# Spectral filter plus expert lookup on one core: the last tile in one piece, and a new list of ranks

## The chip, the cores and the metric

The kernel runs on one core of a Trainium2 chip. The metric is the device time of one execution in microseconds (us); the program must give the reference's output. Times of several runs are given as a median with the lowest and the highest. The profile is of one execution.

## The reference

The input `x` has 2048 rows of 576 columns. The output is `x` plus two branches.

- Branch A is a global spectral filter: a layer norm over the columns, a real two-dimensional Fourier transform over rows and columns, a product with complex weights `w_r + i w_i`, and the inverse transform.
- Branch B is an expert lookup with product keys. Each row is multiplied with query weights for 32 heads; each head's query has two halves of 128, and each half is compared with 8 keys; the best key of each half gives one of 64 experts. With one candidate per head the softmax is 1. The head adds `gelu(x . u[e]) * v[e]`.

```
xn = layernorm(x)
y  = irfft2(rfft2(xn) * (w_r + 1j * w_i))
q  = x @ w_q                      # 32 heads, 2 x 128 each
e  = argmax(q1 @ k1.T) * 8 + argmax(q2 @ k2.T)
out = x + y + sum over heads of gelu(x . u[e]) * v[e]
```

## The kernel before

All transforms are matrix products on TensorE. The rows are split as 64 x 32, and `x` lies in SBUF as 16 tiles of 128 partitions and 576 columns (`XN`, and as `XD` with the columns as two halves). The stages are these.

- Forward: `ln` and `folds` make the normed and folded tiles, `dft128` the first part of the row transform into `AB` and `ABL`.
- Query weights: 32 pieces of `w_q` are loaded and contracted with the keys (`fold_part`), so that the scores come straight from `x`.
- For each of 16 groups: `d_fwd`, `s_fwd`, `s_mul`, `s_inv` (column transform, rest of the row transform, product with the weights `Wt`, inverse row transform). Between them, for each of 8 pairs of tiles, the lookup: `x_t`, `scores`, `route`, `combine`. `combine` writes the expert weights of two tiles into `CAT` (the profile calls it by its storage, `MT`).
- Last stage: for each of 16 tiles `d_inv` gives the inverse column transform (11 + 3 matrix products, folds on ACT, VectorE and GpSimd), and `fin` does the rest: 16 products into one PSUM tile of 128 x 576 (the inverse row transform of 64 with weights `RT` in f32, and `CAT` times `vS` in f16), one VectorE sum with `x` that writes back to `XD`, and two output transfers of 64 partitions, each 144 KB. One f32 product shows as two records in the profile, so a tile has 8 f32 and 12 f16 records.

The output transfers of `fin` go to SyncE's queue; for tiles 13 to 15 the second one goes to ACT's queue. The last tile is different: it is worked in two column halves of 144 of each 288, each with its own PSUM tile, 16 products, one sum and two transfers of 72 KB.

The order of the work is not the order of the program text. Every operation is first recorded in a planner (`_Plan`). `prepare` finds the dependencies, and `forward` then runs a list schedule: at each step the engine that can start earliest takes, of its ready operations, the one with the lowest number in `RANK`, which has one number for each recorded operation (consecutive TensorE calls of one stage may be one operation). Costs of operations come from `cost`: a transfer from SyncE costs

```
            return max(450.0, out.shape[0] * n * size_of(out.dtype) / 400.0), self.land
```

in nanoseconds of its queue, and one from ACT 450. The planner also places the PSUM tiles. Then `issue` emits all operations in that order, from one line (L546), so that almost every instruction of the profile bears this line. `RANK` begins at line 138.

Of the kernel before, what the change touches and what calls it, by code (L numbers as in the profile page):

```python
# [32 lines left out]
def _consts():  # L33
# [168 lines left out]
)  # L202
# [362 lines left out]
def _body(ctx, tc, nc, plan, a, out):  # L565
# [590 lines left out]
    @staged  # L1156
    def fin(t, y):
        x = XD[:, t]
        if t == 15:
            for n, z in enumerate((slice(0, 144), slice(144, 288))):  # L1160
                p = PS("bc"[n])
                for k in range(4):
# [145 lines left out]
```

## Time and profile before

| | |
|---|---|
| median of 3 runs | 213.25 us (212.79 to 215.01) |
| the profiled execution | 213.16 us |
| its span, first to last instruction | 211.4 us |
| TensorE matmul busy | 189.9 us, 90% |
| VectorE busy | 183.6 us, 87% |
| ScalarE (ACT) busy | 129.9 us, 61% |
| GpSimd (POOL) busy | 110.4 us, 52% |
| mean granted TensorE clock | 0.996 |
| output transfers | 28 of 144 KB from SyncE, 2 from ACT; 2 of 72 KB from each |

In the profile's rows PE is the matrix product on TensorE, PEld its weight load, DVE is VectorE, SPq and ACTq are the queues of SyncE and ACT that issue transfers. A row of the timeline has the start, the time to the end of the merged group, the engine, the operation, the tiles (out<-in) and the count. A row of a DMA view has the queue or the engine, the count, the size and the time from issue to landing. The output is called `out_dram`; the last stage's input tiles are `A` and `MT`, its sums write `XN`.

### The profile page before, as it was taken

How to read it: one execution, taken by the hardware profiler on the slowest of the kernel's cores; microseconds unless marked ns; L12 is line 12 of the kernel's file. 1: busy time of each engine (PE TensorE's matmuls, PEld its weight loads, DVE VectorE, ACT ScalarE, POOL GpSimd, SP SyncE). 2: the span in 40 equal slices, each digit the busy share in tenths (PEclk: the TensorE clock that was granted, in tenths of full speed). 3: DMA queues.
4: the chain of work that ended last, by engine and by line, in shares of the span. 5: the costliest groups of instructions: out<-in, count | busy, mean ns of one | idle time of the engine just before them, and what ended most of it. 6: DMA issues, size and time to landing. Idle time of an engine off the chain costs nothing.

```text
span 211.4 us, 6192 instructions
## 1 busy us (share of the span) xinstructions
PE 189.9 (90%) x2408; PEld 130.6 (62%) x2408; DVE 183.6 (87%) x430; ACT 129.9 (61%) x305; POOL 110.4 (52%) x153
## 2 busy tenths in 40 slices
PE   0187799999999999999999999999989999999980
PEld 0175467778767566746666645465644787878850
DVE  2999899955986977988899999999999999999880
ACT  2378998899956884954948974693826622422310
POOL 5526363523088431592518535874836338768750
PEclk9999999999999999999999999999999999999998
DMA  6999999999999999997355062010100001484755
GB/s 197 367 419 410 421 414 416 375 374 399 414 424 407 414 392 401 446 400 302 87 175 158 35 198 67 0 40 0 40 0 2 3 3 28 116 198 113 171 132 150
DMA packets 17453, 48.13 MB, mean 228 GB/s; under 512 B 2192, under 2 KB 8848, under 8 KB 16656
## 3 DMA queue, kind: packets, MB, share of 16 engines
q1 hardware_dynamic: 16848, 47.30, 61.3%
q10 hardware_dynamic: 576, 0.44, 0.7%
q8 instruction: 19, 0.31, 0.6%
q14 instruction: 10, 0.08, 0.1%
HBM read 43.01 MB, written 4.72 MB: 226 GB/s over the span
## 4 chain that ended last, share of the span: by engine, by line
PE 61%; DVE 28%; issue 3%; ACT 2%; DMA 2%; POOL 1%; DVEq 0%; POOLq 0%
PE banks L546 61%; DVE t L546 6%; DVE MT L546 4%; DVE st L546 4%; DVE A L546 3%; DVE w L546 2%; DVE AB L546 2%; DMA XN<-in_x_dram 2%; DVE ABL L546 1%; DVE rr L546 1%; DVE mx L546 1%; DVE mm__96 L546 1%; DVE mv L546 1%; DVE mxr L546 1%; DVE al L546 1%
## 5 line engine op out<-in xcount | busy, mean ns | idle before, releaser
L546 PE MATMUL banks<-MU,xT 128*128 128x512 f16 x192 | 45.6, 379 | 0.6 <-DVE w L546 0.6
L546 PE MATMUL banks<-c,AB 128*128 128x145 f16 (+2 forms) x320 | 37.6, 251 | 0.0
L546 PEld LDWEIGHTS <-xT 128*128 128x128 f16 x224 | 21.1, 98 | 24.5 <-issue 1.5
L546 POOL TENSOR_TENSOR y<-t,t 128x289 f32<-128x289 f32 x32 | 23.8, 766 | 18.4 <-DVE t L546 12.8
L546 POOL TENSOR_TENSOR A<-t 128x287 f32<-128x287 f32 (+2 forms) x42 | 26.2, 641 | 8.8 <-DVE t L546 4.7
L546 POOL TENSOR_TENSOR yh<-y,yh 128x578 f16<-128x578 f32 x16 | 21.2, 1328 | 9.5 <-DVE mxr L546 3.0
L546 POOL TENSOR_TENSOR xT<-xf,xT 128x640 f16<-128x640 f32 x10 | 14.3, 1428 | 22.3 <-DVE A L546 8.2
L546 DVE SCALAR_TENSOR_TENSOR t<-banks,wx,Wt 128x578 f32<-128x578 f32 x32 | 24.6, 811 | 1.4 <-PE banks L546 1.4
L546 PE MATMUL banks<-Rs,yl 128*99 128x128 f32 x64 | 11.0, 305 | 13.0 <-ACT Rs L546 11.2
L546 PE MATMUL banks<-w,KP 128*32 128x288 f32 x256 | 20.5, 415 | 0.3 <-DMA w<-in_wq_dram 0.3
L546 ACT ACTIVATE AB<-banks 128x512 f32<-128x512 f32 (+1 forms) x32 | 18.8, 591 | 0.7 <-PE banks L546 0.7
L546 PE MATMUL banks<-c,ABL 99*128 99x289 f16 (+1 forms) x64 | 18.9, 296 | 0.0
L546 PE MATMUL banks<-Rs,A 128*128 128x128 f32 x128 | 18.7, 297 | 0.0
L546 PEld LDWEIGHTS banks<-c,AB 128*128 128x128 f32 x128 | 18.1, 190 | 0.7
L546 PEld LDWEIGHTS banks<-Rs,yl 128*99 128x99 f32 x64 | 8.3, 180 | 16.5 <-ACT Rs L546 11.9
L546 ACT ACTIVATE yh<-banks 128x290 f32<-128x290 f32 (+1 forms) x16 | 7.2, 457 | 18.2 <-PE banks L546 18.2
L546 PEld LDWEIGHTS banks<-Rs,A 128*128 128x128 f32 x128 | 17.1, 209 | 1.9 <-issue 1.4
L546 DVE TENSOR_REDUCE MT<-w 128x128 bf16<-128x896 bf16 (+1 forms) x16 | 18.1, 1142 | 0.1
L546 POOL TENSOR_TENSOR t<-XN 128x289 f32<-128x289 f32 x14 | 11.5, 824 | 11.4 <-DVE rr L546 3.2
L546 PEld LDWEIGHTS <-AB 128*128 128x128 f16 x192 | 17.0, 146 | 0.1
L546 ACT ACTIVATE A<-banks 128x578 f16<-128x578 f32 (+1 forms) x16 | 10.4, 650 | 8.8 <-PE banks L546 8.8
L546 PE MATMUL banks<-A,s 64*64 64x289 f16 (+1 forms) x320 | 15.6, 336 | 0.0
(131 smaller groups left out, 413.1 us busy)
## 6 DMA issues: line engine op xcount, KB each, us to landing
w<-in_wq_dram SPq DMA_DIRECT2D x32, 576.0 KB, 6.4
xf<-in_xT_dram SPq DMA_DIRECT2D x16, 320.0 KB, 5.2
Wt<-in_W_dram SPq DMA_DIRECT2D x8, 578.0 KB, 6.5
out_dram<-XN SPq DMA_DIRECT2D x28, 144.0 KB, 2.5
XN<-in_x_dram SPq DMA_DIRECT2D x3, 1154.0 KB, 10.3
s<-in_s_dram SPq DMA_DIRECT2D x16, 192.0 KB, 3.5
XN<-in_xd_dram SPq DMA_DIRECT2D x2, 1152.0 KB, 8.3
XN<-in_xd_dram SPq DMA_DIRECT2D x1, 2304.0 KB, 14.0
```

The source lines that it names most:

```text
L546: ins = fn(*[x.place() if isinstance(x, _Ps) else x for x in args], **{k: x.place() if isinstance(x, _Ps) else x for k, x in kw.items()}).ins
```

## The change

`fin` loses its branch for the last tile, so that tile 15 is worked like tile 14: one PSUM tile, 16 products, one sum, and two transfers of 144 KB, the first from SyncE and the second from ACT. This removes four recorded operations of the planner (1273 become 1269), and `RANK` is replaced by a list of 1269 other numbers. The words of the change say that output transfers are counted at their traced issue times in the order; `cost` itself is the same before and after, so of this only the new list is in the code.

```diff
 RANK = (
-    1031, 1229, 1032, 1219, 1241, 1243, 1242, 1033, 1245, 730, 572, 810, 562, 803, 319, 320, 329, 377, 707,
...
+    755, 784, 785, 862, 1225, 1234, 1233, 1238, 1224, 570, 578, 569, 568, 1127, 515, 767, 462, 769, 1084,
...
 )
...
     def fin(t, y):
         x = XD[:, t]
-        if t == 15:
-            for n, z in enumerate((slice(0, 144), slice(144, 288))):
-                p = PS("bc"[n])
-                for k in range(4):
-                    for h in range(2):
-                        hs = slice(64 * h, 64 * h + 64)
-                        for c in range(2):
-                            cs, ds = slice(64 * c, 64 * c + 64), slice(288 * c + z.start, 288 * c + z.stop)
-                            w, m = ((RT[hs], y[hs, ds]) if k == 0 else
-                                    (CAT[hs, t, 64 * (k // 3):64 * (k // 3) + 64], vS[hs, k % 2 ^ 1, ds]))
-                            P.matmul(p[cs, h, z], w, m, start=(k == 0), stop=(k == 3), tile_position=(64 * h, 64 * c))
-                V.scalar_tensor_tensor(x[:, :, z], p[:, :, z], sc[:, 11:12], x[:, :, z], op0=OP.mult, op1=OP.add)
-                for c in range(2):
-                    (A if c else Q).dma_start(os[t, c, :, :, z], x[64 * c:64 * c + 64, :, z])
-            return
         p = PS("bc"[t % 2])
         for k in range(4):
             for h in range(2):
...
```

124 rows, old and new, of the table RANK are left out of this document.

## The prediction

> **What bounds the kernel now.** I read the page first, then the busy time by stage, then the end of the chain of waits, and last the instructions and transfers of the final 8 us one by one.
>
> ```profile
> span 211.4 us, 6192 instructions
> PE 189.9 (90%) x2408; PEld 130.6 (62%) x2408; DVE 183.6 (87%) x430; ACT 129.9 (61%) x305; POOL 110.4 (52%) x153
> ...
> q8 instruction: 19, 0.31, 0.6%
> ```
>
> The stage table gives, after the stretch, its length, each engine's busy time (with its instructions), the granted clock, the DMA share and GB/s.
>
> ```profile
> 0.00:31.25 31.25, 17.94 (x138) 13.71 (x138) 26.04 (x103) 21.66 (x60) 15.71 (x36) 1.00 0.95 371
> 31.25:118.05 86.80, 86.06 (x1087) 59.16 (x1088) 71.96 (x161) 66.50 (x143) 40.66 (x44) 1.00 0.89 344
> 118.05:175.30 57.25, 56.17 (x653) 33.84 (x651) 56.87 (x110) 33.66 (x82) 31.56 (x39) 1.00 0.11 33
> 175.30:205.10 29.80, 29.71 (x532) 23.85 (x532) 27.94 (x58) 8.07 (x23) 22.45 (x35) 1.00 0.53 126
> 205.10:211.40 6.30, 0.00 (x0) 0.00 (x0) 0.78 (x2) 0.00 (x0) 0.00 (x0) 0.86 0.60 164
> ```
>
> Until 31.25 us the loads and VectorE set the pace. From there to 205.10 TensorE is idle for only 0.74 + 1.08 + 0.09 = 1.91 us by the second to fourth rows, and from 118.05 VectorE is idle for only 0.38 + 1.86 = 2.24 us. After 205.10 come 6.30 us in which TensorE does nothing and the DMA engines are 60% busy. So there are two places where an edit can act: a body in which two engines are nearly full, and a tail of transfers.
>
> ```profile
> 175.32 28.86 PE banks L546 x492
> ...
> 204.21 0.46 DVE XN L546
> ...
> 204.95 0.51 DVE XN L546
> 205.46 0.42 DVEq L1304
> ```
>
> The chain runs through the last stage on TensorE and then over the last sums (L546 is the planner's emitting line, so every instruction bears it; the tile names tell them apart). It stops at 205.88, 5.5 us before the span's end, because the view follows no transfer to its landing. Therefore the transfers have to be read one by one.
>
> **The change part by part.** *Product.* These are the last whole tile (t = 14, the first two rows) and the two halves of t = 15:
>
> ```profile
> 203.14 0.66 PE L546 MATMUL banks<-A,c 64*64 64x288 f32 x8
> 203.62 0.55 PE L546 MATMUL banks<-vS,MT 64*64 64x288 f16 x12
> 203.99 0.43 PE L546 MATMUL banks<-A,c 64*64 64x144 f32 x8
> 204.23 0.37 PE L546 MATMUL banks<-vS,MT 64*64 64x144 f16 x12
> 204.42 0.42 PE L546 MATMUL banks<-A,c 64*64 64x144 f32 x8
> 204.67 0.37 PE L546 MATMUL banks<-vS,MT 64*64 64x144 f16 x12
> ```
>
> The whole tile lasts from 203.14 to 204.17, 1.03 us; the halves last from 203.99 to 205.04, 1.05 us. Put in place of the halves, a whole tile ends at 203.99 + 1.03 = 205.02. Twenty matmul records and twenty weight loads go, worth 0.02 us here. ACT and SyncE issue nothing but these transfers at the end (no engine but VectorE is busy after 205.10), so no compute waits behind an issue.
>
> *Sum.* VectorE's rows are the sum of t = 14 and the two half sums:
>
> ```profile
> 204.21 0.82 DVE L546 SCALAR_TENSOR_TENSOR XN<-banks,sc,XN 128x576 f32<-128x576 f32 x1
> ...
> 204.95 0.93 DVE L546 SCALAR_TENSOR_TENSOR XN<-banks,sc,XN 128x288 f32<-128x288 f32 x2
> ```
>
> The halves end at 204.95 + 0.93 = 205.88. The sum of t = 14 starts 0.04 after its product's end at 204.17, so a whole sum would start at 205.06 (VectorE is free at 205.03) and end at 205.06 + 0.82 = 205.88. The difference is nothing. What is lost is the head start of the first half: the chain has it end at 204.95 + 0.51 = 205.46, 0.42 before the second.
>
> *Transfers.* The issues of the tail, with the two queues' times:
>
> ```profile
> 203.71 0.61 SPq L546 DMA_DIRECT2D out_dram<-XN  x1
> 204.21 0.67 ACTq L546 DMA_DIRECT2D out_dram<-XN  x1
> ...
> 205.07 1.90 SPq L546 DMA_DIRECT2D out_dram<-XN  x1
> 205.74 1.24 ACTq L546 DMA_DIRECT2D out_dram<-XN  x1
> 207.06 0.56 SPq L546 DMA_DIRECT2D out_dram<-XN  x1
> 207.08 0.83 ACTq L546 DMA_DIRECT2D out_dram<-XN  x1
> 207.92 0.53 SPq L546 DMA_DIRECT2D out_dram<-XN  x1
> ```
>
> The last four of these are the quarters of t = 15. Two issues, the 1.90 and the 1.24, run long and both end near 206.97. The times from issue to landing, of narrow windows around the issues at 203.14, 203.71, 205.06 with 205.07, and 207.92, are:
>
> ```profile
> out_dram<-XN SPq DMA_DIRECT2D x1, 144.0 KB, 2.3
> ...
> out_dram<-XN SPq DMA_DIRECT2D x1, 144.0 KB, 4.1
> ...
> out_dram<-XN ACTq DMA_DIRECT2D x1, 144.0 KB, 4.0
> out_dram<-XN SPq DMA_DIRECT2D x1, 144.0 KB, 4.4
> ...
> out_dram<-XN SPq DMA_DIRECT2D x1, 72.0 KB, 2.5
> ```
>
> A transfer that meets nothing takes 2.3; the next one lands only at 203.71 + 4.1 = 207.8. Then the landings come at a fixed pitch: four more whole transfers by 205.07 + 4.4 = 209.5 (0.42 each), and four quarters by 207.92 + 2.5 = 210.4 (0.23 each). After that the program needs 211.4 - 210.4 = 1.0 to end. The tail is thus a backlog and not a last transfer. What starts it shows in the DMA queues of the window 204.9 to 205.6:
>
> ```profile
> q1 hardware_dynamic: 141, 0.14, 87.3%
> q8 instruction: 1, 0.02, 12.3%
> ```
>
> One instruction packet takes 0.123 x 16 x 0.7 = 1.38 us on one of the 16 engines, in the middle of the transfers, and every transfer needs its share of that engine. By the page there are 19 such packets of 0.31 MB; over 2408 + 2408 TensorE instructions that is 64 bytes each, so I read them as TensorE's instruction stream, one packet per 253 instructions.
>
> Now the price. Two whole transfers in place of four quarters, behind the same backlog: 2 x 0.42 against 4 x 0.23, that is 0.84 against 0.92, a gain of 0.1. That is the small end. If the lost head start of 0.42 counts in full, the tail loses 0.42 - 0.08 = 0.3. The large end has no packet in the way: the transfers land from 203.71 + 2.3 = 206.0 on at a pitch of 0.42, seven of them, so the last by 206.0 + 6 x 0.42 = 208.5; but the two of t = 15, issued at 205.95, can't land before 205.95 + 2.3 = 208.25 and, one pitch later, 208.7. That is 1.7 earlier than 210.4. Between these I take a gain of 0.9: the packet still comes (40 instructions fewer are a sixth of its pitch), but two of the five whole transfers in the backlog, those of t = 12 or 13, are placed ahead of it (2 x 0.42), and the quarters' 0.1 goes.
>
> The Trainium skill, "DMA: Bandwidth & Descriptors", section "Anatomy of one DMA — SWDGE (gpsimd) path", fits a transfer's time on the GpSimd path by about 2.0 us plus its bytes over 436 GB/s. For 144 KB this gives an estimate of 2.34 us, which the 2.3 of the undisturbed transfer bears out though it is issued from SyncE, and the 4.0 to 4.4 of the backlog do not; by the rule alone the tail would shrink by 2.1 us and the kernel would take 211.0. The same page's "Rules for kernel authors" says to issue a transfer early and let it overlap with compute, which speaks against giving up the early half; by that the kernel would lose the 0.42 and take 213.6.
>
> *The order.* The whole list of ranks is new, so the body can be reordered anywhere. What the profile bounds is the gain: TensorE's 1.91 us of idle time from 31.25 on, or VectorE's 2.24 from 118.05 on. A loss has no such bound; an equal 2.2 us is my estimate from the same rows. I take nothing, because both engines are full and the profile favours neither sign.
>
> The sum: 213.16 us is the profiled execution's own time (span 211.4 and 1.8 around it); 213.16 - 0.9 = 212.3, rounded. The median of the three runs shown, 213.25, is 0.1 away, so the forecast of the median is 212.3 as well.
>
> **The rivals.** *Nothing changes.* The backlog and its packet stay as they are, or the new ranks don't place the output transfers otherwise: in the planner's code a transfer still costs 450 ns (the trace has 0.53 to 0.67 for the undisturbed ones), so "counted at their traced times" can only live in the list. Time: 213.16 - 0.1 = 213.1. For it: sums and product end at the same 205.88.
>
> *Clear tail and a better body.* No packet falls among the last transfers (1.7), and the order recovers half of VectorE's 2.24 us (1.1): 213.16 - 2.8 = 210.4. For it: an edit that shortens TensorE's stream by 40 instructions can drop the packet, if the end of the program no longer reaches its place, and VectorE has idle time before 118.05 (86.80 - 71.96 = 14.8 us) into which routing work can be drawn.
>
> *Slower: the last routing comes late.* The last tiles' f16 products read the routing weights that ACT writes last:
>
> ```profile
> 202.34 0.38 ACT L546 ACTIVATE MT<-banks 128x256 f16<-128x256 f32 x1 [0.88 <-PE banks L546]
> ...
> 203.38 0.49 PEld L546 LDWEIGHTS <-MT 64*64 64x64 f16 x12
> ...
> L546 DVE SCALAR_TENSOR_TENSOR XN<-banks,sc,XN 128x576 f32<-128x576 f32 x15 | 11.7, 810 | 0.3 <-PE banks L546 0.2
> L546 DVE TENSOR_TENSOR t<-banks,yh 128x290 f32<-128x290 f32 x14 | 6.1, 450 | 0.5 <-ACT yh L546 0.4
> ```
>
> They are written by 202.72 and read by t = 14 at 203.38, a slack of 0.66 us. If the new order puts this chain on VectorE behind two more tiles, each with two folds of 0.45 and a sum of 0.81, it comes 2 x 1.71 = 3.4 us later and the end moves by 3.4 - 0.66 = 2.8: 216.0 us. One tile would cost 1.1. It decides from 0.66 us of delay on. Against it: VectorE's idle time in the last stage (1.86) can absorb part.
>
> **How the numbers follow.** Chances: the forecast of 212.3 (a gain under 1%) 0.37; nothing changes, 213.1, 0.22; clear tail and better body, 210.4, 0.27; late routing, 216.0, 0.14. About 1%, 2.1 us around 213.25, is what a measurement of this kernel can tell from no change: three runs spanned 212.79 to 215.01. So faster has 0.27, within 1% 0.59, slower 0.14. The range reaches down past 210.4 by half a microsecond of the body's unknown, to 209.9, and up to 213.1 plus one tile's 1.1 and 0.2 of run spread, 214.4; it leaves the larger losses and the largest gains out.
>
> **What would show it.** Right: the last whole sum ends near 205.9 and is one row of about 0.82; two issues follow it, and the last lands before 209.6; fewer than five whole transfers lie behind the last q8 packet. Wrong in the tail: the last two transfers still take 4 us to land, and the pitch of 0.42 runs to 210.3. Wrong in the body: the last TensorE record lies over 1 us away from 205.1, either way; then VectorE's idle time between 118 and 205 us has changed by as much, and the forecast fails by the term I set to nothing.

## The result and the profile after

The changed kernel takes 214.94 us (median of 15 runs, 212.59 to 216.44), the old one 213.12 (15 runs, 212.78 to 215.49). The ratio is 1.0065, with a 95% interval from 1.0036 to 1.0094: 0.65% slower, where the forecast was 0.4% faster and the range ended at 214.4. The profiled execution of the changed kernel took 216.44 us and is one of five at 216.0 to 216.4 which the ratio leaves out, so the 3.3 us that its span lies above the old one are more than the 1.8 us between the medians, and its profile shows more loss than the usual run has.

The page of the changed kernel, its head lines and three lines of its slices (each digit or figure is a fortieth of the span, 5.4 us):

```profile
span 214.7 us, 6159 instructions
PE 191.7 (89%) x2388; PEld 132.9 (62%) x2388; DVE 182.2 (85%) x429; ACT 130.9 (61%) x305; POOL 110.0 (51%) x153
...
PEclk9996789999999999999999999999999999999997
DMA  6999949999999999999632533101100000566566
GB/s 176 377 418 416 363 124 344 420 409 379 414 426 410 420 411 385 434 403 422 197 120 76 182 114 92 55 0 40 37 5 0 3 0 5 137 146 146 131 149 184
```

The engines do less work, as the change says: twenty products and one sum fewer. But two things are new, and both lie in the first 33 us: the granted clock dips in slices 4 to 6, and the loads, which run at some 410 GB/s, fall to 124 in the sixth slice. The old page has this:

```profile
PEclk9999999999999999999999999999999999999998
DMA  6999999999999999997355062010100001484755
GB/s 197 367 419 410 421 414 416 375 374 399 414 424 407 414 392 401 446 400 302 87 175 158 35 198 67 0 40 0 40 0 2 3 3 28 116 198 113 171 132 150
```

Next the chain of waits of the changed kernel, its long stretches on TensorE (start, length, what):

```profile
92.07 39.91 PE banks L546 x474
...
179.54 29.57 PE banks L546 x512
...
209.20 0.82 DVE XN L546
```

In the old kernel a stretch begins at the same place in the work, after the last routing step that needs loaded query weights:

```profile
87.68 30.34 PE banks L546 x345
```

So the changed kernel is 92.07 - 87.68 = 4.39 us late there, 179.54 - 175.32 = 4.22 at the start of the last stage, 210.02 - 205.88 = 4.14 at the end of the last sum, and 3.3 at the end of the span. All of the loss in this profile arises before 92 us, the body after it gives 0.25 back, and the tail 0.8. Three kernels below with the same list, whose profiled executions took 214.4 to 214.6 us, are 2.0 to 2.2 us late at the same place.

**The head.** The busy time by stage (stretch, length, PE, PEld, DVE, ACT, POOL, granted clock, DMA share, GB/s), old kernel first:

```profile
0.00:80.00 80.00, 66.21 (x793) 49.05 (x797) 64.50 (x203) 61.96 (x148) 36.99 (x60) 1.00 0.99 389
15.00:20.00 5.00, 2.73 (x24) 2.01 (x24) 4.97 (x19) 4.15 (x12) 2.98 (x5) 1.00 1.01 407
25.00:30.00 5.00, 4.95 (x48) 3.29 (x48) 4.48 (x16) 4.66 (x14) 2.65 (x6) 1.00 1.03 418
35.00:80.00 45.00, 44.52 (x620) 32.40 (x622) 34.71 (x89) 36.83 (x80) 19.80 (x22) 1.00 1.01 399
```

and the changed one:

```profile
0.00:80.00 80.00, 63.53 (x684) 48.05 (x686) 60.60 (x197) 58.84 (x142) 36.77 (x60) 0.96 0.94 367
15.00:20.00 5.00, 2.42 (x14) 2.23 (x13) 5.00 (x25) 3.36 (x10) 0.52 (x1) 0.78 1.02 416
25.00:30.00 5.00, 5.00 (x38) 4.04 (x37) 4.24 (x17) 4.35 (x16) 2.84 (x9) 0.69 0.38 116
35.00:80.00 45.00, 44.43 (x556) 31.98 (x556) 33.87 (x95) 36.85 (x84) 20.61 (x23) 1.00 1.02 410
```

In the old kernel the DMA engines are full through the first 80 us (share 0.99). In the changed one they are full after 35 us too, so what they missed in the hole at 25 to 30 us they don't make up by 80 us. The arithmetic closes: (389 - 367) GB/s over 80 us is 1.76 MB, and at 0.41 MB per us, the rate of full engines in these rows, that is 4.3 us, against the 4.39 of the chain.

TensorE closes it as well, for in these rows it is as full from 35 us on as the loads are (44.52 and 44.43 of 45.00 us). Its busy time from 35 us to the end, in the old kernel, the changed one and the changed one with its pauses filled (below):

```profile
35.00:211.40 176.40, 168.19 (x2235) 113.91 (x2233) 153.80 (x316) 104.75 (x237) 93.18 (x115) 1.00 0.56 198
35.00:214.70 179.70, 172.55 (x2260) 116.81 (x2258) 155.47 (x327) 108.94 (x247) 93.85 (x116) 0.99 0.58 207
35.00:212.50 177.50, 170.32 (x2239) 115.20 (x2237) 153.73 (x321) 107.10 (x240) 92.83 (x115) 1.00 0.57 203
```

The changed kernel has 172.55 - 168.19 = 4.36 us more of TensorE's work left there, against 4.39 late, and the filled one 2.13, against 2.17. So the head falls behind in two things that are both full afterwards, bytes loaded and products done, and neither sum says which of them sets the pace.

How the loads reach the chain is seen in the products of the key tile `KP` with the query weights `w`. The view of one tile gives count, duration, first and last start; old kernel, then changed:

```profile
L546 PE MATMUL banks<-w,KP x256: 406/406/430, 19.5 to 83.3; 128*32 128x288 f32 x128
L546 POOL TENSOR_TENSOR KP<-kT x4: 208/209/387, 5.5 to 6.2; 128x14 f32<-128x14 f32 x4
```

```profile
L546 PE MATMUL banks<-w,KP x256: 406/406/431, 28.0 to 87.7; 128*32 128x288 f32 x128
L546 POOL TENSOR_TENSOR KP<-kT x4: 213/214/216, 26.1 to 26.9; 128x14 f32<-128x14 f32 x4
```

The same 256 products take 63.8 us in the one and 59.7 in the other, but the changed order starts them 8.5 us later and ends them 4.4 later; the long stretch of the chain begins 4.4 us after the last of them in both (83.3 to 87.68, 87.7 to 92.07). Blocks of `w` stay in their buffers until these products have read them, so the next loads of `w` wait on SyncE's queue. The waits of that queue between 17 and 40 us (total, times, longest), changed kernel:

```profile
SPq L546 <- PE banks L546: 13.4, 5, 7.5
```

The old kernel has 12.0 us of this too, but in eight waits, the longest 2.5; what is new is one wait of 7.5. Around it the queue issues nothing for 8.6 us, until just after the first of these products at 28.04:

```profile
19.89 0.33 SPq L546 DMA_DIRECT2D s<-in_s_dram  x1
28.80 5.13 SPq L546 DMA_DIRECT2D w<-in_wq_dram  x5
```

And TensorE in that stretch, changed kernel (start, busy, tiles, idle before):

```profile
18.03 1.17 PE L546 MATMUL banks<-Rs,yl 128*99 128x128 f32 x4 [2.58 <-ACT Rs L546]
...
24.50 1.05 PE L546 MATMUL banks<-Rs,yl 128*99 128x128 f32 x4 [2.03 <-ACT Rs L546]
...
28.04 1.18 PE L546 MATMUL banks<-w,KP 128*32 128x288 f32 x16
```

Two pauses of 2.58 and 2.03 us between the head's transforms, which the old order partly fills with products of `w` (its first start at 19.45). The granted clock follows the pauses:

```profile
17.83:21.24 3.41, 3.21 (x15) 3.21 (x16) 3.41 (x12) 1.49 (x5) 1.45 (x3) 0.50 1.03 416
21.24:24.66 3.42, 1.39 (x12) 1.20 (x11) 2.79 (x10) 3.35 (x10) 1.46 (x3) 1.00 1.03 413
24.66:28.07 3.41, 3.41 (x20) 3.14 (x20) 3.02 (x12) 2.76 (x9) 2.28 (x8) 0.50 0.47 188
```

Two windows of 3.41 us at half clock, with a whole one between them; the old profile has none after 15 us until the end. The Trainium skill, "TensorE: Matmul & The Clock Gate", section "What's actually happening", gives such windows, 3.41 us long and at half or full rate only, and the trace agrees. It has the clock fall after an idle window; here pauses of 2.58 and 2.03 us, shorter than a window, went before.

**The tail.** Times to landing, from narrow windows around the issues at 207.78 and 210.58, and the instruction queue's share in the window 209.1 to 209.4, changed kernel:

```profile
out_dram<-XN SPq DMA_DIRECT2D x1, 144.0 KB, 3.6
...
out_dram<-XN SPq DMA_DIRECT2D x1, 144.0 KB, 3.2
...
q8 instruction: 1, 0.02, 21.5%
```

The last sum is one row of 0.82 (209.20 to 210.02). The backlog begins to land at 207.78 + 3.6 = 211.4 and ends at 210.58 + 3.2 = 213.8, seven whole transfers at a pitch of 0.40. From the last sum to the last landing there are 3.8 us, where the old kernel had 210.42 - 205.88 = 4.54.

### The profile page after: what moved, and what is told of

Same layout as the page of the kernel before. It is cut to its first block, busy times and chain, and to the rows that moved or that the text cites. A ratio compares the mean times of both kernels' runs of the same rounds, so it can differ in the third digit from the quotient of the medians.

```text
span 214.7 us, 6159 instructions
## 1 busy us (share of the span) xinstructions
PE 191.7 (89%) x2388; PEld 132.9 (62%) x2388; DVE 182.2 (85%) x429; ACT 130.9 (61%) x305; POOL 110.0 (51%) x153
## 4 chain that ended last, share of the span: by engine, by line
PE 63%; DVE 22%; ACT 6%; DMA 2%; issue 2%; POOL 1%; SPq 0%; DVEq 0%; ACTq 0%
PE banks L546 63%; DVE t L546 5%; DVE MT L546 5%; DVE w L546 3%; DMA XN<-in_x_dram 2%; ACT t L546 2%; DVE st L546 2%; DVE A L546 1%; ACT AB L546 1%; DVE AB L546 1%; DVE mx L546 1%; ACT Rs L546 1%; DVE ABL L546 1%; POOL A L546 1%; DVE rr L546 1%
## 5 line engine op out<-in xcount | busy, mean ns | idle before, releaser
L546 PE MATMUL banks<-MU,xT 128*128 128x512 f16 x192 | 45.1, 379 | 0.0
L546 POOL TENSOR_TENSOR y<-t,t 128x289 f32<-128x289 f32 x32 | 22.6, 725 | 20.7 <-DVE t L546 13.0
L546 POOL TENSOR_TENSOR A<-t 128x287 f32<-128x287 f32 (+2 forms) x42 | 27.4, 668 | 9.9 <-DVE t L546 4.8
L546 PE MATMUL banks<-Rs,yl 128*99 128x128 f32 x64 | 12.7, 337 | 16.0 <-ACT Rs L546 15.8
L546 PEld LDWEIGHTS banks<-Rs,yl 128*99 128x99 f32 x64 | 9.7, 205 | 20.0 <-ACT Rs L546 17.7
L546 DVE TENSOR_TENSOR ABL<-banks,ABL 33x256 f16<-33x256 f32 x32 | 13.1, 411 | 9.1 <-ACT ABL L546 7.2
L546 PE MATMUL banks<-Rs,A 128*128 128x128 f32 x128 | 19.5, 305 | 0.0
L546 PEld LDWEIGHTS banks<-Rs,A 128*128 128x128 f32 x128 | 18.0, 219 | 1.9 <-DVE t L546 0.5
```

The lines of the kernel that those rows point to most:

```text
L546: ins = fn(*[x.place() if isinstance(x, _Ps) else x for x in args], **{k: x.place() if isinstance(x, _Ps) else x for k, x in kw.items()}).ins
```

## The experiments

Two accounts of the loss stood against each other at first: the single piece, or the order. Later ones are about the order: that the halved clock alone makes the loss (the clock account), that the late key tile does (the keys account), or that the loads missed in the head do, whichever item of the order makes them pause. No run separates this last account from that of TensorE's work left over from the head. The table gives every run, with the profiled execution's load rate over the first 80 us, the start of the long stretch of the chain, and the 3.41 us windows at half clock between 15 and 55 us.

| kernel | median us (range) | ratio to before [95%] | GB/s 0 to 80 us | long stretch starts | half-clock windows |
|---|---|---|---|---|---|
| before | 213.12 (212.78 to 215.49) | 1 | 389 | 87.68 | 0 |
| after | 214.94 (212.59 to 216.44) | 1.0065 [1.0036, 1.0094] | 367 | 92.07 | 2 |
| old order, one piece | 212.80 (211.77 to 215.01) | 0.9986 [0.9967, 1.0005] | 389 | 87.62 | 0 |
| new order, halves | 215.36 (214.59 to 217.11) | 1.0114 [1.0084, 1.0144] | 378 | 89.69 | 1 |
| old head to 45 us, new rest | 215.33 (213.82 to 216.53) | 1.0095 [1.0061, 1.0130] | 363 | 92.49 | 2 |
| new head to 45 us, old rest | 217.47 (216.37 to 218.05) | 1.0199 [1.0174, 1.0224] | 361 | 93.68 | 2 |
| after, both pauses filled | 214.34 (213.55 to 214.94) | 1.0050 [1.0032, 1.0068] | 378 | 89.85 | 0 |
| old order, one piece, pauses filled | 212.40 (212.16 to 212.71) | 0.9962 [0.9946, 0.9978] | 389 | 87.58 | 0 |
| after, first pause filled | 214.55 (213.75 to 215.18) | 1.0056 [1.0034, 1.0078] | 378 | 89.92 | 1 |
| after, keys early | 215.78 (215.38 to 216.26) | 1.0118 [1.0083, 1.0152] | 370 | 91.26 | 1 |
| keys and first products early | 216.63 (214.43 to 217.19) | 1.0120 [1.0067, 1.0173] | 365 | 92.33 | 3 |
| the same, first pause filled | 215.50 (213.82 to 217.77) | 1.0088 [1.0062, 1.0114] | 369 | 91.56 | 1 |
| old order to 100 us, new rest | 212.91 (212.58 to 213.40) | 0.9971 [0.9950, 0.9992] | 388 | 87.91 | 1 |
| new order to 100 us, old rest | 217.25 (216.23 to 217.79) | 1.0178 [1.0148, 1.0208] | 368 | 91.71 | 2 |

### The two halves of the change, each alone

The old list of ranks for all operations that stay (without the four that the single piece drops), and the last tile in one piece:

```diff
 RANK = (
-    755, 784, 785, 862, 1225, 1234, 1233, 1238, 1224, 570, 578, 569, 568, 1127, 515, 767, 462, 769, 1084,
...
+    1031, 1229, 1032, 1219, 1241, 1243, 1242, 1033, 1245, 730, 572, 810, 562, 803, 319, 320, 329, 377, 707,
...
```

> The last tile in one piece, with the old list of ranks (its four removed operations cut out): the fin edit alone. In the profiles the last sum to last landing took 210.42 - 205.88 = 4.54 us before and 213.75 - 210.02 = 3.73 us after, 0.81 less. Theory HEAD (the new order loses its time in the first 45 us, where the granted clock is halved twice and the loads pause; the fin edit gains): about 0.8 us faster than before, ratio 0.996. Rival TAIL (the edit itself costs, its gain in the profile of after comes from the new order's spacing of the transfers): 0 to 0.4 us slower, ratio 1.000 to 1.002. If the backlog and its instruction packet stay, as the record's smallest case has it: 0.1 faster.

The new list, and the column halves kept, with ranks for the four operations beside those of tile 15:

```diff
     def fin(t, y):
         x = XD[:, t]
+        if t == 15:
+            for n, z in enumerate((slice(0, 144), slice(144, 288))):
...
```

> The new list of ranks with the last tile still in two column halves: the order alone. Theory HEAD: the order loses more than the whole change does, since the gain of the single piece is missing: 1.0065 + 0.004 = ratio 1.010, 2 us slower than before. Rival TAIL: the order is neutral or better, ratio 0.998 to 1.003.

The single piece alone gave 0.9986 and the order alone 1.0114, 2.4 us. With the new order the single piece is worth 1.0114 - 1.0065 = 0.5%, 1.0 us, though the two intervals overlap; with the old one 0.14%, whose interval reaches no change. So the loss is the order's, and the gain of the single piece is small and by itself not clear of nothing. The tail of the single piece with the old order, first all transfers issued from 203.1 us on, then the two of tile 15:

```profile
out_dram<-XN SPq DMA_DIRECT2D x5, 144.0 KB, 3.0
out_dram<-XN ACTq DMA_DIRECT2D x3, 144.0 KB, 2.7
...
out_dram<-XN SPq DMA_DIRECT2D x1, 144.0 KB, 3.4
out_dram<-XN ACTq DMA_DIRECT2D x1, 144.0 KB, 3.2
```

This tail holds no packet of the instruction queue, as the large end of the forecast's range for the tail supposed. The span is 210.3, 1.1 shorter than before, and not 1.7: the first two rows are medians, and without a packet the transfers still take 2.4 us for the first and up to 3.6 behind it, 3.4 and 3.2 for the last two, instead of 2.3.

### Is it the head? Two orders joined at 45 us

The list of one kernel up to a planned time, and of the other from there:

```diff
+CUT = 45000.0
...
+        (first, t1), (rest, t2) = plan_of(HEAD), plan_of(RANK)
+        n = next(k for k, i in enumerate(first) if t1[i] >= CUT)
+        head = set(first[:n])
+        order = first[:n] + [i for i in rest if i not in head]
```

> The changed kernel, but every operation that the old order starts in its planned first 45 us is issued in the old order, and the rest in the new one: the new head undone. Theory HEAD: no halved clock between 15 and 31 us, no pause of the loads, and the whole loss is gone: ratio 0.996 like the tail alone. Rival BODY (the loss arises after 45 us, and the late head is absorbed in slack): ratio stays at 1.006 or above.

> The mirror image: the new order for the first 45 us, the old order for the rest, last tile in one piece. Theory HEAD: as slow as the changed kernel, ratio 1.006 to 1.010, with the halved clock in its head. Rival BODY: ratio 0.996, as the fin edit alone.

Both came out slower, and say nothing on the question. The seam made a stall of its own: by my reading, the loads that one list had already placed were queued ahead of a block of `w` that the other needed. In the kernel with the old head the chain has the first row below, which neither original has (L510 is its emitting line), and TensorE stands still for 2.94 us until that load has landed (second row); the other kernel's chain has a like row of 6.97 us:

```profile
41.19 7.96 DMA w<-in_wq_dram
...
49.20 0.69 PE L510 MATMUL banks<-w,KP 128*32 128x288 f32 x8 [2.94 <-DMA w<-in_wq_dram]
```

Both also load less in the first 80 us than either original (363 and 361 GB/s), and are the latest of all at the long stretch.

### Is it the clock? Pauses filled with unread products

These kernels add work: products into columns of the following product's PSUM tile that nobody reads, put into TensorE's pauses of the head. Nothing is left out. 41 of them fill both pauses of the changed kernel, 19 the first alone, and 23 those of the old order:

```diff
+            if 12000.0 <= end < 31000.0 and start[k] - end > 400:
+                n[k] = int((start[k] - end) * 1.1 / 115.0)
...
+            mm(out[:, c:c + 256], w, x, start=True, stop=True)
```

> The changed kernel with 41 products that nobody reads (128 x 256 of zeros, f16, into columns of PSUM that no tile uses) put into the two long pauses of TensorE in the head: 19 ahead of the third tile's transform and 22 ahead of the fifth's. Nothing else moves. Theory CLOCK (the pauses make the granted clock fall to a half for windows of 3.41 us, each of which costs about 2 us): the clock is whole from 15 us on and the kernel takes what its order and its tail allow, ratio 0.996 to 0.999. Rival ORDER (the pauses are only a sign of late loads and late folds; the halved clock costs nothing by itself): ratio stays at 1.006 or rises by the products' own time.

> The changed kernel with the 19 products of the first pause alone. Theory CLOCK: the first halved window goes and the second stays: about half the loss is left, ratio 0.999 to 1.004, and a profile with one halved window at 24 to 28 us. Rival ORDER: no change against the changed kernel, 1.006.

> The old order with the last tile in one piece, and the same products in its three pauses (23 of them). Theory CLOCK: the profile of before has no halved window after 15 us, so nothing is to be gained in an undisturbed run: ratio 0.998, like the fin edit alone; this is the control for the cost of the products. Rival ORDER: the products cost their own time, ratio 1.002 or more.

With both pauses filled the clock is whole, and the loss is still there: 1.0050, whose interval overlaps that of 1.0065, so that no gain is shown. What went is the spread (213.55 to 214.94, where the changed kernel runs from 212.59 to 216.44). The stretch starts at 89.85 instead of 92.07, but the 92.07 is from the one profile of the changed kernel, at 216.44 us. The hole in the loads is smaller but not closed:

```profile
25.00:30.00 5.00, 4.64 (x52) 2.97 (x51) 5.00 (x19) 4.97 (x16) 2.94 (x10) 1.00 0.83 278
```

378 GB/s over 80 us against 389 are 0.88 MB, 2.1 us, and the stretch starts 89.85 - 87.68 = 2.17 late. So the clock account is not enough by itself. The runs of the changed kernel say the same: at the same mean granted clock of 0.979, one took 214.47 us and another 216.44. Filling the first pause alone leaves one halved window and the same lateness, 2.24. With the old order the filled kernel is 0.9962, the fastest of all, narrow and ahead of both originals; whether the filling adds anything to the single piece is within the intervals.

### Is it the late key tile?

In the changed kernel the keys' load is the thirteenth on SyncE's queue, issued at 9.13 and landed 12.3 us later, and `KP` is built at 26.1. In the first kernel below the load is put fourth (operation 7) and `KP` is built ahead of the third fold (14 to 17); in the second three groups of products of `w` and `KP` (319, 321, 323) are put ahead of the fifth tile's transform as well; in the third the first pause of that is filled with 19 unread products:

```diff
+        ahead([7], 3)
+        ahead([14, 15, 16, 17], 74)
```

> The changed kernel with two things moved ahead and nothing else: the load of the keys kT goes from the ninth place or later of SyncE's queue to the fourth, and GpSimd's four KP operations, which need it, go ahead of the third tile's fold. TensorE's order stays. Theory LOADS (the query-weight loads pause because their buffers are freed late, by the first KP products; TensorE's order puts these behind the fifth tile's transform): a small part of the loss goes, as KP was ready only 0.5 us after TensorE came to its products in the run with filled pauses, ratio 1.003 to 1.006. Rival KEYS (the late keys alone cause the pause): the whole loss goes, ratio 0.996 to 0.998.

```diff
+        ahead([321, 319], 133)
+        ahead([323], 145)
```

> As the run before, and three KP products (of the first two query-weight blocks, and of the third one) go ahead of the fifth tile's transform on TensorE, where the old order has such products. Theory LOADS: the buffers come free some 4 us earlier, the DMA engines don't pause between 25 and 31 us, and the loss goes but for a halved clock window that may still come from the first pause: ratio 0.996 to 1.000. Rival BODY (the loss after all lies behind 35 us): 1.005.

> The run before with 19 unread products in TensorE's first pause, so that the clock stays whole. Theories LOADS and CLOCK together: ratio 0.995 to 0.998, the same as the old order with the last tile in one piece (0.9962 with filled pauses). If the new order after 35 us is worse by itself, 0.5% or more above that.

None of them is faster than the changed kernel: 1.0118, 1.0120, 1.0088. The keys account falls: in the first of them `KP` is built at 10.1 us, and its first product still starts only at 26.7, where TensorE's order has it. The account of the missed loads fell short here too: it expected at most 1.006 of the first, 1.000 of the second and 0.998 of the third. The last of the three shows where its loss went. Its hole at 25 to 30 us is gone, but one has opened later:

```profile
25.00:30.00 5.00, 4.68 (x48) 3.08 (x40) 5.00 (x20) 4.77 (x16) 2.29 (x5) 1.00 1.03 413
30.00:35.00 5.00, 2.90 (x16) 1.68 (x16) 3.59 (x11) 4.93 (x15) 3.13 (x5) 0.73 0.88 358
35.00:40.00 5.00, 5.00 (x50) 4.10 (x47) 3.45 (x15) 3.02 (x8) 1.42 (x3) 0.93 0.77 266
```

With 369 GB/s over 80 us, 1.6 MB or 3.9 us are missing, and its stretch starts 3.88 late.

### The seam where the loads are over

The two orders joined once more, at a planned 100 us instead of 45, behind nearly all loads:

```diff
-CUT = 45000.0
+CUT = 100000.0
```

> The changed kernel, but what the old order starts in its planned first 100 us is issued in the old order, and the rest in the new one. The seam lies behind the stretch in which the DMA engines are full, so that no load is queued wrongly over it, as happened with the seam at 45 us. Theory LOADS (all that the new order loses, it loses by bytes not loaded in the first 80 us, at 1 us per 0.41 MB): 389 GB/s over the first 80 us, and the loss gone, ratio 0.995 to 0.999. Rival LATE (the order after 100 us has a loss of its own): 1.003 or more.

> The mirror image: the new order for the first 100 us, the old one after, the last tile in one piece. Theory LOADS: as slow as the changed kernel, ratio 1.004 to 1.009, with 365 to 379 GB/s over the first 80 us. Rival LATE: 0.995 to 0.999.

With the old order for the first 100 us and the new one behind it, the loss is gone: 0.9971, 388 GB/s, 0.23 us late. The mirror keeps it, and more than the 1.009 expected at most: 1.0178. Its profile is 4.03 us late at the stretch and 179.67 - 175.32 = 4.35 at the start of the last stage, so that the seam adds 0.3; why all of its runs (216.23 and above) are slower than the changed kernel's median isn't shown. The kernel with the old order ahead also has a halved window (15.93 to 19.34), which costs nothing to be seen here, where the loads don't pause behind it. The loss is thus placed in the first 100 us of the order, and the part of the new order behind them is about as good as the old (0.9971 beside 0.9986, with overlapping intervals).

## Why the prediction was wrong, point by point

*The terms of product and sum, set to nothing:* right. The last sum is one row of 0.82, two issues follow it, and no engine waits longer for them.

*The tail, a gain of 0.9 between -0.3 and 1.7:* right in size, in part by luck. The profiled tail gave 4.54 - 3.76 = 0.8, and between runs the single piece was worth 0.3 us (old order, not clear of nothing) to 1.0 (new order). The reason given for the size was wrong: two whole transfers should have gone ahead of the packet, and none did. Five transfers of earlier tiles still land behind it, as before. Of the 0.8, about 0.6 is that the backlog begins to land 211.38 - 210.02 = 1.36 us after the last sum instead of 207.81 - 205.88 = 1.93; the packet takes 0.215 x 16 x 0.3 = 1.0 us here and took 1.38 there. The rest is mostly two whole transfers at a pitch of 0.40 in place of four quarters at 0.23. Two rules were weighed in that part. The one by bytes and a fixed time (the Trainium skill, "DMA: Bandwidth & Descriptors", section "Anatomy of one DMA — SWDGE (gpsimd) path") gave 211.0 and is not borne out for transfers in a backlog: the last two took 3.3 and 3.2 us, and 3.2 and 3.4 without the packet, not 2.34. Nor is the loss of 0.42 borne out that the same page's advice to issue early (section "Rules for kernel authors") would give: the old order with the single piece measured 0.9986, up to 1.0005 by its interval, and 0.42 us would be 1.002.

*The order, taken as nothing:* this is the step that failed. The prediction weighed the order only by the idle time of two engines that it called full, TensorE from 31.25 us on and VectorE from 118.05 on, and read the first stage as one in which the loads and VectorE set the pace. By its own row TensorE idles for 31.25 - 17.94 = 13.31 us of that stage, and how much of TensorE's work and of the loads an order brings into the head was given no price. The runs showed in its place that the new order alone costs 2.4 us, and that the kernels with its head fall behind there: with the pauses filled, 2.13 us more of TensorE's work is left at 35 us and 0.88 MB less is loaded by 80 us; in the changed kernel's own profile it is 4.36 us and 1.76 MB. The quoted rows also had a DMA share of 0.95 to 31.25 and 0.89 for the next 86.8 us, an average that hides a share of 1.0 until 80 us at least (the row of 35 to 80 above): the loads were a third full resource, and what is missing at 80 us goes with 2.4 us of delay per MB. Over the fourteen profiles the start of the long stretch follows the bytes of the first 80 us, from 389 GB/s and 87.6 to 361 and 93.7, whatever the clock did and wherever the hole was. The gain was bounded by 2.2 us and the loss put at an equal 2.2 by symmetry; the new order alone measured 2.4. That the two agree is luck, since the 2.2 is VectorE's idle time behind 118 us, and the loss arose before 92. That loss was then left out of the range: 212.3 + 2.2 would have been 214.5, near the 214.94.

*The rivals.* "Nothing changes" and "clear tail and a better body" did not come. The slower rival had the right sign and the wrong place: no routing step is late for the last tiles, as TensorE is busy for 29.55 of the last stage's 29.66 us (the second of these rows of the stage table, changed kernel):

```profile
118.05:179.54 61.49, 60.78 (x674) 36.06 (x673) 61.00 (x118) 39.07 (x92) 35.61 (x43) 1.00 0.16 46
179.54:209.20 29.66, 29.55 (x512) 23.62 (x512) 27.68 (x57) 7.67 (x23) 22.66 (x35) 1.00 0.53 127
```

*What would show it.* The test named for a wrong body was met: the last TensorE record lies 4.1 us late. But the sign expected with it, a change of VectorE's idle time from 118 us on, did not come: it was 2.24 us and is (61.49 - 61.00) + (29.66 - 27.68) = 2.47 by these rows.

*What stays open.* Whether the loads or TensorE's own work set the pace behind the head isn't separated, as both are full there. Which decision in the new head opens the hole isn't settled: moving the keys, `KP` and three groups of products moved the hole and didn't close it. Nor is it settled why the kernels with no halved window and with one (89.85, 89.69 and 89.92) are equally late, and the changed kernel with two, in its one profile, is 2.2 us later. And that the pauses cause the halved clock is seen only by its going when they are filled; a profile with the old head has such a window too (15.93 to 19.34).

## What to carry to other kernels

Where a list of orders is replaced as a whole, the stage to look at first is the one whose resource can't catch up. Split the page's average shares until each stretch has one limit; here the loads are full until 80 us and TensorE from 35 us on, so what either misses ahead of that has no later place to go. When a transfer queue pauses, look for the buffers it waits for and for the engine that has not yet read them. And carry a bound that you call symmetric into the range.

## What the runs showed of the hardware

Work that nobody reads did no harm and may help: the kernel with 23 unread products has the narrowest spread of all (212.16 to 212.71), and 41 of them took both halved windows out of the changed order. What a halved window costs is not shown by itself: nothing is to be seen of it in one profile (388 GB/s), and the one profile with the new order and two of them is 2.2 us later than those with one or none. Output transfers of 144 KB behind the first of the tail took 4.0 to 4.4 us to landing in the old kernel and 3.2 to 3.9 in the changed one, both with an instruction packet among them, and 2.5 to 3.6 where none fell; the last two took 3.3 and 3.2 with the packet, and 3.2 and 3.4 without it.
